# Two routings cut into lists of small steps, and gathers and first splits tied to dense groups, in a fused attention and two-MoE kernel

## The chip, the cores and the metric

The kernel runs on one core of one Trainium2 chip. The metric is the device time of one execution in microseconds (us). The engines are named as in the profile: PE multiplies matrices, ACT applies activation functions and copies, DVE and POOL work elementwise, SP issues DMAs. Each engine works through its own queue in order, and engines wait for each other by semaphores. POOL also issues the indirect DMAs (gathers and scatters).

## The reference

```python
attn_out = phi(q) (phi(k)^T v) / (phi(q) z + 1e-6)       # phi(x) = [exp(p), exp(-p)], p = x w_phi - max|x w_phi|
x = attn_out laid out as 2304 x 512
x = (silu(x @ w_gate) * (x @ w_val)) @ w_out             # first MoE: one dense block, 512 -> 1536 -> 512
logits = x @ w_gate2; e = argmax(logits)                 # second MoE: 8 experts, each token goes to one
out[token] = gate_weight * sigmoid((x @ w_output_gate)[e]) * (relu(x @ w1[e]) @ w2[e])
```

## The kernel before

Attention runs unit by unit and is woven into the first MoE by a planned order. The first MoE works on 6 blocks of 384 tokens (`n`), each in 12 slices (`f`) of the hidden width. A slice is three dense groups on PE: `mm_gv(n, f, 0)` (12 products of 128x384, called G here), `mm_gv(n, f, 1)` (the same for the value half, V) and `mm_o` of the slice before (9 products of 128x512, called o here). Every product is made of two-part numbers, so each weight is split: ACT makes the high part (L520) and POOL the low part (L524), three uses ahead, in a ring of four buffers. Between the groups, ACT takes the tanh (L547), DVE multiplies G (L550) and V (L553), ACT cuts the high part (L556) and DVE the low part (L559) for o. G and V have one PSUM bank each, so the next slice's G waits for L550, and the next V for L559.

The second MoE sorts the tokens by expert into slots of 128 rows. Slots 0 to 7 hold only tokens of blocks 0 to 4, so that they can start early: while PE is in block 5, `route_early` counts the tokens by expert (DVE), `slot_map` makes the row lists of the slots (PE, DVE), `gather` fetches the rows of a slot (POOL), and `load_w` fetches an expert's weights (SP). After block 5, `route_late` does the same for the remaining tokens, beside the first slots. Per slot there are `xt` (transpose of the gathered rows), `l1` (first layer, four chunks of weights), `ht`, and `l2` (four chunks). `Chunks.split` cuts each chunk of 128x1024 weights into two parts: ACT L889 the high one, DVE L890 the low one, in a ring of five.

The small steps are kept in a list `todo`, and `fill(1)` runs one entry of it after a dense group; an entry that is one big function is emitted as a whole. Emission is not execution: outside the planned order a scheduler places the instructions, by their data dependencies and the place in the program. In the program of before it put the four gathers of slots 0 to 3 in a row on POOL, and the first three weight splits of slot 0 into the middle of block 5, though gathers 1, 2, 3 and these splits are emitted at different places:

```python
todo += [(totals, (EARLY_T,)), (route_early, ()), (load_w, (0, 0)),
         (idle, ()), (idle, ()), (early, ())]
```

Of the kernel before, what the change touches and what calls it, by code (L numbers as in the profile page):

```python
# [13 lines left out]
AF = mybir.ActivationFunctionType  # L14
ALU = mybir.AluOpType
# [7 lines left out]
NTILE = NT // P  # L23
# [7 lines left out]
NES = 8  # L31
NLS = 17
# [149 lines left out]
def kernel(ctx, tc, qT, kT, v1, wphi, w1cat, wlog, mw1, mw2, consts, out):  # L182
    nc = tc.nc
    PE, ACT, DVE, POOL, SP = nc.tensor, nc.scalar, nc.vector, nc.gpsimd, nc.sync
# [21 lines left out]
    cv = {}  # L206
# [15 lines left out]
    IDX = buf(NES + NLS).bitcast(I32)  # L222
# [3 lines left out]
    NSI = EXI[:, 28:32]  # L226
    TKE = buf(8)
    S1, S2, S3, S4 = (buf(NTILE) for _ in range(4))
    NB, E1, E2, E3, E4 = (buf(8) for _ in range(5))
# [16 lines left out]
    T1, T2, T3 = (A[:, st + 464 + i * 312:st + 776 + i * 312] for i in range(3))  # L246
# [18 lines left out]
    x2d = dp.tile([NT, ROW], F32, name="x2d")  # L265
# [194 lines left out]
    for u in range(QSW, 16):  # L460
# [3 lines left out]
        x = qk(u + 1)  # L464
# [66 lines left out]
    def gv_mm(n, f, which):  # L531
        ps = PS[:, GB + which, :BT]
        i = where[n, f, which]
        wh, wl = WH[i % 4], WL[i % 4]
        for k in range(4):
            c = slice(k * P, (k + 1) * P)
            xh, xl = XH[:, n % 3, k, :], XL[:, n % 3, k, :]
            PE.matmul(ps, wh[:, c], xh, start=(k == 0), stop=False)  # L538
            PE.matmul(ps, wh[:, c], xl, start=False, stop=False)  # L539
            PE.matmul(ps, wl[:, c], xh, start=False, stop=(k == 3))  # L540

    def mm_gv(n, f, which):
        gv_mm(n, f, which)
# [152 lines left out]
    def bc(ap, n):  # L696
        return ap.rearrange("p (j o) -> p j o", o=1).to_broadcast([P, ap.shape[1], n])

    def bm(ap, n):
        return ap.rearrange("p (o e) -> p o e", o=1).to_broadcast([P, n, ap.shape[1]])  # L700

    def v3(ap, j, e):
        return ap[:, :j * e].rearrange("p (j e) -> p j e", e=e)

    def tt(out_, a, b, op):
        DVE.tensor_tensor(out=out_, in0=a, in1=b, op=op)

    def rsum(out_, a):
        DVE.tensor_reduce(out=out_, in_=a, axis=AX.X, op=ALU.add)
# [65 lines left out]
    def excl(out_, a):  # L775
        w = v3(T1, 8, 8)
        tt(w, cv["m8"].rearrange("p (e f) -> p e f", f=8), bm(a, 8), ALU.mult)
        rsum(out_, w)

    def pick(out_, a, nt):  # L780
        w = v3(T1, nt, 8)
        tt(w, OH[:, 0:nt, :], bm(a, nt), ALU.mult)
        rsum(out_, w)
# [6 lines left out]
    def slot_columns(q, nt, ns, valid):  # L790
        ng = 3 if valid else 2
        eq = v3(T1, nt, ns)
        tt(eq, bm(cv["iota"][:, 0:ns], nt), bc(q, ns), ALU.is_equal)
        q2 = Q2[:, :nt * ng * ns].rearrange("p (j g s) -> p j g s", g=ng, s=ns)
        DVE.tensor_scalar(out=q2[:, :, 0, :], in0=eq, scalar1=cv["pidx"], scalar2=None, op0=ALU.mult)
        tt(q2[:, :, 1, :], eq, bc(cv["jidx"][:, 0:nt], ns), ALU.mult)
        if valid:
            DVE.tensor_copy(q2[:, :, 2, :], eq)
# [16 lines left out]
    def experts(ends, ns, s0):  # L815
        w = v3(T1, ns, 8)
        tt(w, bm(ends, ns), bc(cv["iota"][:, s0:s0 + ns], 8), ALU.is_le)
        rsum(EXF[:, s0:s0 + ns], w)
        DVE.tensor_scalar(out=EXF[:, s0:s0 + ns], in0=EXF[:, s0:s0 + ns], scalar1=7.0, scalar2=None, op0=ALU.min)
        DVE.tensor_copy(EXI[:, s0:s0 + ns], EXF[:, s0:s0 + ns])  # L820
        a = max(s0, 2)
        tt(T3[:, a:s0 + ns], EXF[:, a:s0 + ns], EXF[:, a - 2:s0 + ns - 2], ALU.not_equal)
        DVE.tensor_copy(CHI[:, a:s0 + ns], T3[:, a:s0 + ns])

    EARLY_T = 15

    def route_early():
        nt = EARLY_T
        w = v3(T1, 8, 18)
        tt(w, bc(NB, 18), bm(cv["thge"], 8), ALU.is_ge)  # L830
        rsum(E1, w)
        excl(E2, E1)
        DVE.tensor_scalar(out=E3, in0=E2, scalar1=-1.0, scalar2=float(NES), op0=ALU.mult, op1=ALU.add)
        DVE.scalar_tensor_tensor(out=TKE, in0=E3, scalar=0.0, in1=E1, op0=ALU.max, op1=ALU.min)
        tt(E4, E2, TKE, ALU.add)
        experts(E4, NES, 0)
        q, tk, ge, r = S1[:, 0:nt], S2[:, 0:nt], S3[:, 0:nt], RK[:, 0:nt]
        pick(q, E2, nt)
        pick(tk, TKE, nt)
        tt(ge, r, tk, ALU.is_ge)  # L840
        tt(q, q, r, ALU.add)
        DVE.scalar_tensor_tensor(out=q, in0=ge, scalar=1000.0, in1=q, op0=ALU.mult, op1=ALU.add)
        slot_columns(q, nt, NES, False)

    def route_late():
        nt = NTILE
        w = v3(T1, 8, 18)
        tt(w, bc(NB, 18), bm(cv["thgt"], 8), ALU.is_gt)
        rsum(E1, w)
        tt(E1, E1, TKE, ALU.subtract)  # L850
        excl(E2, E1)
        tt(E3, E2, E1, ALU.add)
        DVE.tensor_copy(NSI[:, 0:1], E3[:, 7:8])
        DVE.tensor_scalar(out=E4, in0=E3, scalar1=float(NES), scalar2=None, op0=ALU.add)
        experts(E4, NLS, NES)
        tt(E2, E2, TKE, ALU.subtract)
        q, tk, lt, r = S1[:, 0:nt], S2[:, 0:nt], S3[:, 0:nt], RK[:, 0:nt]
        pick(q, E2, nt)
        pick(tk, TKE, nt)
        tt(lt, r, tk, ALU.is_lt)  # L860
        tt(q, q, r, ALU.add)
        DVE.scalar_tensor_tensor(out=q, in0=lt, scalar=1000.0, in1=q, op0=ALU.mult, op1=ALU.add)
        slot_columns(q, nt, NLS, True)


    R = [A[:, offs["KR"]:offs["KR"] + 8192], A[:, offs["WR"]:offs["WR"] + 8192]]
# [10 lines left out]
    XG = []  # L877
    HB, HTB, XB, YB = [3, 4], [5, 6], 7, [0, 1]

    class Chunks:  # L880
# [3 lines left out]
        def split(self, n):  # L884
            while self.done < min(n, len(self.seq)):
                s, c = self.seq[self.done]
                src = R[s % 2][:, c * 1024:(c + 1) * 1024]
                h, l = RG[self.done % NR]
                ACT.activation(h, src, AF.Copy)  # L889
                DVE.tensor_tensor(out=l, in0=src, in1=h.bitcast(F32), op=ALU.subtract)  # L890
                self.done += 1

# [4 lines left out]
    def load_w(s, part):  # L897
        e = SP.value_load(EXI[0:1, s:s + 1], min_val=0, max_val=NE - 1)
        src = (mw1 if part == 0 else mw2)[ds(e, 1)].rearrange("o p c -> (o p) c")
        kw = {}  # L900
        if s >= 2:
            kw["cond"] = SP.value_load(CHI[0:1, s:s + 1], min_val=0, max_val=1)
        SP.dma_start(out=R[s % 2][:, part * 4096:(part + 1) * 4096], in_=src, **kw)

    def gather(s):
        rows = EARLY_T * P if s < NES else NT
        POOL.indirect_dma_start(out=XG[s % 4], out_offset=None, in_=x2d[0:rows, :],
                                in_offset=IndirectOffsetOnAxis(ap=IDX[:, s:s + 1], axis=0),
                                bounds_check=rows - 1, oob_is_err=False)

    def xt(s):
        ps = PS[:, XB, :]
# [99 lines left out]
    def post(n):  # L1012
        ops = []
        for t in range(3):
            ops += [(post_log, (n, t)), (post_mm, (n, t))]
        return ops + [(route_a, (n,)), (route_b, (n,))]

    def early():
        slot_map(EARLY_T, NES, 0, False)
        t = ov.tile([P, OVN], F32, name="ov_gather", tag="ov")  # L1020
        for s in range(4):
            XG.append(t[:, s * 520:s * 520 + ROW])
            POOL.memset(XG[s], 0.0)
        gather(0)
        gather(1)
        load_w(0, 1)

    def idle():
        pass

    def fill(n):
        while todo and n > 0:
# [4 lines left out]
    todo = []  # L1037
    for n in range(1, NBLK):
        s0, s1 = pos[0], max(need[n], pos[0])
        for f in range(NFT):  # L1040
            def pace(g):
                run_to(s0 + ((s1 - s0) * (3 * f + g) + 35) // 36)
                if g != 2 or n == 5:
                    fill(1)
            mm_gv(n, f, 0)
            act_g(n, f)
            pace(1)
            mm_gv(n, f, 1)
            act_v(n, f)
            pace(2)  # L1050
            if prev is not None:
                mm_o(*prev)
                if prev[1] == NFT - 1:
                    for t in range(3):
                        post_x2(prev[0], t)
                    todo += post(prev[0])
                    if prev[0] == 4:
                        todo += [(totals, (EARLY_T,)), (route_early, ()), (load_w, (0, 0)),
                                 (idle, ()), (idle, ()), (early, ())]
            prev = (n, f)  # L1060
            pace(3)
            if n == 5 and f == 10:
                xt(0)
            if n == 5 and f == 10:
                load_w(1, 0)
                load_w(1, 1)
    mm_o(*prev)
    for t in range(3):
        post_x2(5, t)
    state["banks"] = [2]  # L1070
    todo += post(5) + [(totals, (NTILE,)), (route_late, ()), (idle, ()), (slot_map, (NTILE, NLS, NES, True))]
    ch = Chunks()

    def mid(n):
# [54 lines left out]
```

## Time and profile before

| | |
|---|---|
| device time, median of 3 runs | 920.05 us (918.99 to 921.12) |
| profiled execution, its own time | 920.25 us |
| span of the profile | 918.5 us |
| PE busy | 894.5 us (97%) |
| DVE busy | 577.0 us (63%) |
| ACT busy | 559.4 us (61%) |
| POOL busy | 393.0 us (43%) |

PE products overlap in the profile: one 128x512 product shows as about 0.40 us, and the next starts 0.23 us after it. So PE counts as busy as soon as products follow each other, and lost time is read from the distance between two starts.

### The profile page before, as it was taken

What the parts mean: (1) busy time and instruction counts of PE and PEld (TensorE: products, weight loads), DVE (VectorE), ACT (ScalarE), POOL (GpSimd) and SP (SyncE); (2) the same over time, 40 slices, a digit from 0 to 9 for tenths busy, and PEclk for the clock granted to TensorE, in tenths of its full rate; (3) what the DMA queues carried; (4) which work ended last, traced back from release to release, by engine and by line L of the source; (5) the groups of instructions that cost most, each with busy time, mean ns of one, the idle gap of its engine ahead of it and who ended that gap; (6) DMA issues with size and microseconds to landing.
All of it is one profiled execution on the core that took longest, in us unless ns stands there. A gap on an engine that the chain in (4) does not pass through costs nothing. (4 is left out here: it accounts for less than half of the span.)

```text
span 918.5 us, 18395 instructions
## 1 busy us (share of the span) xinstructions
PE 894.5 (97%) x7256; PEld 784.8 (85%) x7258; DVE 577.0 (63%) x977; ACT 559.4 (61%) x975; POOL 393.0 (43%) x318
## 2 busy tenths in 40 slices
PE   8899999999999999999999999979999999999995
PEld 6789989999998998898899999969877888888884
DVE  6999776443336435445433422772699988888993
ACT  5878775544353545544444444334688899888883
POOL 1667989445543434433345566566101111112200
PEclk9999999999999999999999999999999999999998
DMA  8767543200020111110000000090001147166240
GB/s 231 221 176 216 168 143 101 62 16 1 2 76 5 38 42 27 50 42 1 2 2 35 1 1 35 2 375 39 35 24 48 47 161 284 30 224 228 64 172 10
DMA packets 20940, 78.90 MB, mean 86 GB/s; under 512 B 5358, under 2 KB 5614, under 8 KB 19056
## 3 DMA queue, kind: packets, MB, share of 16 engines
q1 hardware_dynamic: 17280, 67.60, 22.8%
q0 software_dynamic: 3200, 9.48, 3.1%
q8 instruction: 59, 0.97, 0.4%
q10 hardware_dynamic: 368, 0.59, 0.3%
q14 instruction: 33, 0.27, 0.1%
HBM read 123.23 MB, written 10.00 MB: 145 GB/s over the span
## 5 line engine op out<-in xcount | busy, mean ns | idle before, releaser
L524 POOL TENSOR_TENSOR arena_r<-arena,arena_r 128x512 fp32r<-128x512 f32 x216 | 278.7, 1294 | 246.7 <-ACT arena_r L520 239.3
L520 ACT ACTIVATE arena_r<-arena 128x512 fp32r<-128x512 f32 x216 | 136.2, 631 | 229.3 <-PE banks L539 139.7
L538 PE MATMUL banks<-arena_r 128*128 128x384 f32 x576 | 202.4, 351 | 4.2 <-DVE arena L550 4.1
L890 DVE TENSOR_TENSOR arena_r<-arena,arena_r 128x1024 fp32r<-128x1024 f32 x160 | 193.1, 1255 | 20.3 <-ACT arena_r L889 18.9
L540 PE MATMUL banks<-arena_r 128*128 128x384 f32 x576 | 194.2, 337 | 0.0
L539 PE MATMUL banks<-arena_r 128*128 128x384 f32 x576 | 193.9, 337 | 0.0
L889 ACT ACTIVATE arena_r<-arena 128x1024 fp32r<-128x1024 f32 x160 | 161.9, 1067 | 18.4 <-PE banks L924 10.9
L550 DVE SCALAR_TENSOR_TENSOR arena<-arena,banks 128x384 f32<-128x384 f32 x72 | 39.7, 552 | 130.1 <-ACT arena L547 129.8
L924 PE MATMUL banks<-arena_r 128*128 128x512 f32 x480 | 117.0, 396 | 0.0
L538 PEld LDWEIGHTS banks<-arena_r 128*128 128x128 f32 x576 | 108.6, 189 | 9.5 <-DVE arena L550 4.9
L952 POOL DMA_INDIRECT out_dram<-arena x20 | 20.7, 1037 | 218.9 <-ACT arena L951 218.9
L539 PEld LDWEIGHTS banks<-arena_r 128*128 128x128 f32 x576 | 108.9, 189 | 1.2
L540 PEld LDWEIGHTS banks<-arena_r 128*128 128x128 f32 x576 | 108.7, 189 | 0.0
L924 PEld LDWEIGHTS banks<-arena_r 128*128 128x128 f32 x480 | 88.2, 188 | 20.3 <-ACT arena_r L916 2.1
L576 PE MATMUL banks<-arena_r 128*128 128x512 f32 x216 | 87.6, 405 | 0.0
L577 PE MATMUL banks<-arena_r 128*128 128x512 f32 x216 | 85.1, 394 | 1.0 <-POOL arena_r L524 1.0
L578 PE MATMUL banks<-arena_r 128*128 128x512 f32 x216 | 84.9, 394 | 0.0
L553 DVE TENSOR_TENSOR banks<-arena,banks 128x384 f32<-128x384 f32 x72 | 40.4, 561 | 44.8 <-PE banks L540 44.1
L946 PE MATMUL banks<-arena_r 128*128 128x512 f32 x160 | 62.7, 392 | 1.0 <-ACT arena_r L889 0.7
L948 PE MATMUL banks<-arena_r 128*128 128x512 f32 x160 | 62.4, 390 | 0.0
L947 PE MATMUL banks<-arena_r 128*128 128x512 f32 x160 | 62.4, 390 | 0.0
L318 DVE TENSOR_REDUCE arena<-banks 128x6 f32<-128x768 f32 x48 | 45.8, 954 | 23.6 <-PE banks L310 22.7
(119 smaller groups left out, 1327.2 us busy)
## 6 DMA issues: line engine op xcount, KB each, us to landing
arena<-mw SPq DMA_DIRECT2D x40, 2048.0 KB
ov_conv<-w1cat SPq DMA_DIRECT2D x24, 512.0 KB
arena<-w1cat SPq DMA_DIRECT2D x12, 512.0 KB
arena<-v SPq DMA_DIRECT2D x16, 325.0 KB
x2d<-arena SPq DMA_DIRECT2D x18, 256.0 KB
arena<-qT SPq DMA_DIRECT2D x15, 288.0 KB
arena<-kT SPq DMA_DIRECT2D x15, 288.0 KB
ov_gather<-x2d,arena POOLq DMA_INDIRECT x20, 4.3
```

The lines of the kernel that those rows point to most:

```text
L520: ACT.activation(WH[i % 4], WR[f][w], AF.Copy)
L524: POOL.tensor_tensor(out=WL[i % 4], in0=WR[f][w], in1=WH[i % 4].bitcast(F32), op=ALU.subtract)
L538: PE.matmul(ps, wh[:, c], xh, start=(k == 0), stop=False)
L539: PE.matmul(ps, wh[:, c], xl, start=False, stop=False)
L540: PE.matmul(ps, wl[:, c], xh, start=False, stop=(k == 3))
L576: PE.matmul(ps, GH[f % 2][:, ts_], woh, start=(f == 0), stop=False)
L577: PE.matmul(ps, GH[f % 2][:, ts_], wol, start=False, stop=False)
L578: PE.matmul(ps, GL[f % 2][:, ts_], woh, start=False, stop=(f == NFT - 1))
L889: ACT.activation(h, src, AF.Copy)
L890: DVE.tensor_tensor(out=l, in0=src, in1=h.bitcast(F32), op=ALU.subtract)
L924: PE.matmul(PS[:, HB[h], :], lhs, w[:, h * 512:(h + 1) * 512], start=a, stop=b)
L946: PE.matmul(ps, HTH[:, k, :], wh[:, cs], start=(k == 0), stop=False)
```

## The change

`tt` returns its instruction. `gv_mm` stores the last product of each dense G or V group in `state["pe"]`, and `tie(x)` gives the scheduler (not the chip: there is no semaphore in it) an order, x after that product. `route_early` and `route_late` no longer emit their steps in one call but return lists of small functions that `fill` runs one by one; the early list also holds `totals` and the load of slot 0's first weights. Three of the early steps are tied. Gathers 1, 2 and 3 are tied, and gather 1 is no longer emitted with gather 0 but in slice 10 of block 5, with the loads of slot 1. The high parts of slot 0's first three chunks are tied, so they come after block 5's last V group.

```diff
-            PE.matmul(ps, wl[:, c], xh, start=False, stop=(k == 3))
+            state["pe"] = PE.matmul(ps, wl[:, c], xh, start=False, stop=(k == 3)).ins
...
+    def tie(x):
+
+        tc.add_manual_dep(x.ins, state["pe"].name, mybir.DependencyInfo(
+            mybir.DependencyClass.NoSync, mybir.DependencyReason.SCHED_ONLY), reason="pace")
...
     def route_early():
+
         nt = EARLY_T
-        w = v3(T1, 8, 18)
-        tt(w, bc(NB, 18), bm(cv["thge"], 8), ALU.is_ge)
...
+        def counts():
+            w = v3(T1, 8, 18)
+            tie(tt(w, bc(NB, 18), bm(cv["thge"], 8), ALU.is_ge))
+            rsum(E1, w)
+            excl(E2, E1)
...
+        def picks():
+            pick(q, E2, nt)
+            pick(tk, TKE, nt)
...
+        return [(totals, (nt,)), (counts, ()), (taken, ()), (experts, (E4, NES, 0)), (load_w, (0, 0)), (picks, ()),
+                (place, ()), (slot_columns, (q, nt, NES, False))]
...
+        return [(totals, (nt,)), (counts, ()), (ends, ()), (experts, (E4, NLS, NES)), (picks, ()), (place, ()),
+                (slot_columns, (q, nt, NLS, True)), (idle, ()), (slot_map, (nt, NLS, NES, True))]
...
-                ACT.activation(h, src, AF.Copy)
+                a = ACT.activation(h, src, AF.Copy)
+                if s == 0 and c < 3:
+                    tie(a)
...
+        if 1 <= s <= 3:
+            tie(g)
...
         gather(0)
-        gather(1)
         load_w(0, 1)
...
-                        todo += [(totals, (EARLY_T,)), (route_early, ()), (load_w, (0, 0)),
-                                 (idle, ()), (idle, ()), (early, ())]
+                        todo += route_early() + [(idle, ()), (idle, ()), (early, ())]
...
             if n == 5 and f == 10:
+                gather(1)
                 load_w(1, 0)
                 load_w(1, 1)
...
-    todo += post(5) + [(totals, (NTILE,)), (route_late, ()), (idle, ()), (slot_map, (NTILE, NLS, NES, True))]
+    todo += post(5) + route_late()
```

The queue of DVE, in the middle of the early routing, reads so before (L706 is the helper `tt`, L709 a row sum, L820 and L823 the casts of `experts`, L842 the last step before `slot_columns`):

```order
L819 TENSOR_SCALAR arena<-arena 128x8
L706 TENSOR_TENSOR arena<-arena 128x120
L820 CAST arena<-arena 128x8
L706 TENSOR_TENSOR arena<-arena 128x6
...
L706 TENSOR_TENSOR arena<-arena 128x15
L842 SCALAR_TENSOR_TENSOR arena<-arena 128x15
L706 TENSOR_TENSOR arena<-arena 128x120
L550 SCALAR_TENSOR_TENSOR arena<-arena,banks 128x384
```

And so with the change, where line numbers have moved (L824, L825, L828 are the steps that were L819, L820, L823; L714 is the row sum):

```order
L824 TENSOR_SCALAR arena<-arena 128x8
L706 TENSOR_TENSOR arena<-arena 128x120
L550 SCALAR_TENSOR_TENSOR arena<-arena,banks 128x384
L825 CAST arena<-arena 128x8
L706 TENSOR_TENSOR arena<-arena 128x6
L714 TENSOR_REDUCE arena<-arena 128x15
L828 CAST arena<-arena 128x6
L706 TENSOR_TENSOR arena<-arena 128x120
L706 TENSOR_TENSOR arena<-arena 128x15
L553 TENSOR_TENSOR banks<-arena,banks 128x384
L714 TENSOR_REDUCE arena<-arena 128x15
L559 TENSOR_TENSOR arena_r<-banks,arena_r 128x384
```

The dense step L550 moved ahead of ten small steps (L820 to the last 128x120 product), and the rest of the routing now stands between the dense steps of two further slices.

POOL's queue from the clearing of the gather buffers on, before:

```order
L1023 MEMSET ov_gather 128x516 x4
L524 TENSOR_TENSOR arena_r<-arena,arena_r 128x512 x54
L907 DMA ov_gather<-x2d,arena 128x516 x4
L524 TENSOR_TENSOR arena_r<-arena,arena_r 128x512 x17
L952 DMA out_dram<-arena 2304x512
```

With the change (L936 is the gather, L983 the scatter):

```order
L1054 MEMSET ov_gather 128x516 x4
L524 TENSOR_TENSOR arena_r<-arena,arena_r 128x512 x59
L936 DMA ov_gather<-x2d,arena 128x516
L524 TENSOR_TENSOR arena_r<-arena,arena_r 128x512 x10
L936 DMA ov_gather<-x2d,arena 128x516
L524 TENSOR_TENSOR arena_r<-arena,arena_r 128x512 x2
L936 DMA ov_gather<-x2d,arena 128x516 x2
L983 DMA out_dram<-arena 2304x512
```

Gather 0 moved behind five more low parts (L524), gather 1 behind fifteen, and gathers 2 and 3 behind all seventeen.

ACT's queue at the end of block 5, before; of the splits L889, three stand further up, in the middle of the block:

```order
L547 ACTIVATE arena<-banks 128x384
L889 ACTIVATE arena_r<-arena 128x1024 x2
L556 ACTIVATE arena_r<-banks 128x384
L714 ACTIVATE arena<-banks 128x512 x3
L889 ACTIVATE arena_r<-arena 128x1024 x3
```

With the change (L916 is the split, L719 the copy of block 5's result):

```order
L547 ACTIVATE arena<-banks 128x384
L916 ACTIVATE arena_r<-arena 128x1024 x2
L556 ACTIVATE arena_r<-banks 128x384
L916 ACTIVATE arena_r<-arena 128x1024 x3
L719 ACTIVATE arena<-banks 128x512 x3
L916 ACTIVATE arena_r<-arena 128x1024 x3
```

Three splits more now stand here, ahead of the copies; DVE's low parts follow in the same order.

## Rows read from the trace of the kernel before

**Rows 1.** Windows: busy us of each engine (instructions), PEclk, DMA share, GB/s

```profile
598.00:622.00 24.00, 18.84 (x100) 16.42 (x99) 17.04 (x20) 9.16 (x16) 15.17 (x12) 0.93 0.96 393
618.10:621.30 3.20, 3.20 (x11) 3.20 (x11) 0.89 (x2) 1.01 (x2) 1.28 (x1) 0.50 0.99 415
```

**Rows 2.** Timeline (start, length, what, idle before), PE, two ordinary slices apart

```profile
625.77 0.33 PE L538 MATMUL banks<-arena_r 128*128 128x384 f32 x1
...
638.30 0.33 PE L538 MATMUL banks<-arena_r 128*128 128x384 f32 x1
```

**Rows 3.** Timeline, the early routing on DVE and the first gap

```profile
596.72 0.16 DVE L820 CAST arena<-arena 128x8 int32<-128x8 f32 x1
...
597.37 1.31 POOL L524 TENSOR_TENSOR arena_r<-arena,arena_r 128x512 fp32r<-128x512 f32 x1 [0.79 <-ACT arena_r L520]
...
597.79 0.93 DVE L706 TENSOR_TENSOR arena<-arena 128x15 f32<-128x15 f32 x1
...
598.43 0.40 PE L578 MATMUL banks<-arena_r 128*128 128x512 f32 x1
...
599.16 0.55 DVE L550 SCALAR_TENSOR_TENSOR arena<-arena,banks 128x384 f32<-128x384 f32 x1
...
599.76 0.45 PE L538 MATMUL banks<-arena_r 128*128 128x384 f32 x1 [0.94 <-DVE arena L550]
```

**Rows 4.** Timeline, the products of the slot lists, and the first gather on POOL

```profile
601.96 0.54 PE L804 MATMUL banks<-arena 128*128 128x16 bf16 x15
...
604.61 1.25 POOL L907 DMA_INDIRECT ov_gather<-x2d,arena  x1 [0.33 <-DVE arena L813]
```

**Rows 5.** Timeline, the other gaps of PE and what DVE and POOL did

```profile
608.56 0.34 PE L540 MATMUL banks<-arena_r 128*128 128x384 f32 x1
...
609.03 0.44 PE L538 MATMUL banks<-arena_r 128*128 128x384 f32 x1
...
610.60 6.70 DVE L890 TENSOR_TENSOR arena_r<-arena,arena_r 128x1024 fp32r<-128x1024 f32 x1 [0.25 <-ACT arena_r L889]
...
611.23 0.40 PE L576 MATMUL banks<-arena_r 128*128 128x512 f32 x1
611.24 4.97 POOL L524 TENSOR_TENSOR arena_r<-arena,arena_r 128x512 fp32r<-128x512 f32 x4
612.58 0.50 PE L577 MATMUL banks<-arena_r 128*128 128x512 f32 x1 [0.95 <-POOL arena_r L524]
...
614.07 0.40 PE L577 MATMUL banks<-arena_r 128*128 128x512 f32 x1
614.30 0.39 PE L578 MATMUL banks<-arena_r 128*128 128x512 f32 x1
...
617.82 0.56 PE L538 MATMUL banks<-arena_r 128*128 128x384 f32 x1 [3.13 <-DVE arena L550]
```

**Rows 6.** Timeline, PE, the first product of the group after that

```profile
621.58 0.34 PE L538 MATMUL banks<-arena_r 128*128 128x384 f32 x1
```

**Rows 7.** Timeline, DVE, the V half of an ordinary slice

```profile
642.68 0.56 DVE L553 TENSOR_TENSOR banks<-arena,banks 128x384 f32<-128x384 f32 x1 [0.60 <-PE banks L540]
...
643.81 0.56 DVE L559 TENSOR_TENSOR arena_r<-banks,arena_r 128x384 fp32r<-128x384 f32 x1 [0.56 <-ACT arena_r L556]
```

**Rows 8.** Timeline, DVE and ACT where block 5 ends

```profile
649.94 2.36 DVE L890 TENSOR_TENSOR arena_r<-arena,arena_r 128x1024 fp32r<-128x1024 f32 x2
...
652.21 0.55 DVE L559 TENSOR_TENSOR arena_r<-banks,arena_r 128x384 fp32r<-128x384 f32 x1
...
653.43 1.57 ACT L714 ACTIVATE arena<-banks 128x512 f32<-128x512 f32 x3 [2.20 <-PE banks L578]
...
655.83 0.69 DVE L723 COPY arena<-banks 128x512 f32<-128x512 f32 x1 [3.06 <-PE banks L722]
```

**Rows 9.** DMA issues from 598 to 622 us (count, median us to landing)

```profile
ov_gather<-x2d,arena POOLq DMA_INDIRECT x4, 11.4
```

**Rows 10.** Timeline, PE, the transposes of slot 1

```profile
661.38 0.66 PE L914 MATMUL banks<-arena,ov_gather 128*128 128x128 f32 x4
```

More of the change, by code (lines that the diff above doesn't have):

```diff
@@ L705, in tt @@
     def tt(out_, a, b, op):
-        DVE.tensor_tensor(out=out_, in0=a, in1=b, op=op)
+        return DVE.tensor_tensor(out=out_, in0=a, in1=b, op=op)
+    def tie(x):
+        tc.add_manual_dep(x.ins, state["pe"].name, mybir.DependencyInfo(
+            mybir.DependencyClass.NoSync, mybir.DependencyReason.SCHED_ONLY), reason="pace")
     def rsum(out_, a):
@@ L825, with idle @@
     EARLY_T = 15
+    def idle():
+        pass
     def route_early():
         nt = EARLY_T
-        w = v3(T1, 8, 18)
-        tt(w, bc(NB, 18), bm(cv["thge"], 8), ALU.is_ge)
[L831 to L836, printed above, removed]
-        q, tk, ge, r = S1[:, 0:nt], S2[:, 0:nt], S3[:, 0:nt], RK[:, 0:nt]
@@ L838, in route_early @@
[L838 to L843, printed above, removed]
+        q, tk, ge, r = S1[:, 0:nt], S2[:, 0:nt], S3[:, 0:nt], RK[:, 0:nt]
+        def counts():
[3 more added lines that the diff above has]
+            excl(E2, E1)
@@ new lines, in taken, with place @@
+        def taken():
+            tie(DVE.tensor_scalar(out=E3, in0=E2, scalar1=-1.0, scalar2=float(NES), op0=ALU.mult, op1=ALU.add))
+            DVE.scalar_tensor_tensor(out=TKE, in0=E3, scalar=0.0, in1=E1, op0=ALU.max, op1=ALU.min)
+            tt(E4, E2, TKE, ALU.add)
+        def picks():
+            pick(q, E2, nt)
+            pick(tk, TKE, nt)
+        def place():
+            tie(tt(ge, r, tk, ALU.is_ge))
+            tt(q, q, r, ALU.add)
+            DVE.scalar_tensor_tensor(out=q, in0=ge, scalar=1000.0, in1=q, op0=ALU.mult, op1=ALU.add)
@@ L845, in route_late @@
+        return [(totals, (nt,)), (counts, ()), (taken, ()), (experts, (E4, NES, 0)), (load_w, (0, 0)), (picks, ()),
+                (place, ()), (slot_columns, (q, nt, NES, False))]
     def route_late():
         nt = NTILE
[L847 to L854, printed above, removed]
@@ L855, in route_late, with counts @@
-        experts(E4, NLS, NES)
-        tt(E2, E2, TKE, ALU.subtract)
-        q, tk, lt, r = S1[:, 0:nt], S2[:, 0:nt], S3[:, 0:nt], RK[:, 0:nt]
[L858 to L863, printed above, removed]
+        q, tk, lt, r = S1[:, 0:nt], S2[:, 0:nt], S3[:, 0:nt], RK[:, 0:nt]
+        def counts():
+            w = v3(T1, 8, 18)
+            tt(w, bc(NB, 18), bm(cv["thgt"], 8), ALU.is_gt)
+            rsum(E1, w)
+            tt(E1, E1, TKE, ALU.subtract)
+            excl(E2, E1)
@@ new lines, in ends, with picks, place @@
+        def ends():
+            tt(E3, E2, E1, ALU.add)
+            DVE.tensor_copy(NSI[:, 0:1], E3[:, 7:8])
+            DVE.tensor_scalar(out=E4, in0=E3, scalar1=float(NES), scalar2=None, op0=ALU.add)
+        def picks():
+            tt(E2, E2, TKE, ALU.subtract)
+            pick(q, E2, nt)
+            pick(tk, TKE, nt)
+        def place():
+            tt(lt, r, tk, ALU.is_lt)
+            tt(q, q, r, ALU.add)
+            DVE.scalar_tensor_tensor(out=q, in0=lt, scalar=1000.0, in1=q, op0=ALU.mult, op1=ALU.add)
@@ L906, in gather @@
         rows = EARLY_T * P if s < NES else NT
-        POOL.indirect_dma_start(out=XG[s % 4], out_offset=None, in_=x2d[0:rows, :],
-                                in_offset=IndirectOffsetOnAxis(ap=IDX[:, s:s + 1], axis=0),
-                                bounds_check=rows - 1, oob_is_err=False)
+        g = POOL.indirect_dma_start(out=XG[s % 4], out_offset=None, in_=x2d[0:rows, :],
+                                    in_offset=IndirectOffsetOnAxis(ap=IDX[:, s:s + 1], axis=0),
+                                    bounds_check=rows - 1, oob_is_err=False)
+        if 1 <= s <= 3:
+            tie(g)
     def xt(s):
@@ L1024, in early @@
         gather(0)
-        gather(1)
         load_w(0, 1)
-    def idle():
-        pass
     def fill(n):
```

## Prediction

> **What bounds the kernel now.** I read the busy time by stretch first, then the timeline of the stretch that stood out, on every engine. From 598 to 622 us PE works 18.84 of 24.00 us [rows 1], though in the ordinary slices behind it one product follows the other. What such a slice costs: two G groups, two slices apart, start at 625.77 and 638.30 [rows 2], so a slice takes 6.265 us. Two 128x512 products start 0.23 apart (614.07, 614.30 [rows 5]); nine of them are 2.07, which leaves 4.195 for the 24 products of 128x384, 0.175 each. So the kernel is bound by PE, and the change can only win what PE loses in places, above all in these 24 us.
>
> PE loses it five times there, each read as the distance of two starts less the ordinary one:
> 1. 598.43 to 599.76, where G waits for DVE's L550 [rows 3]: 1.33 - 0.23 = 1.10.
> 2. 608.56 to 609.03 [rows 5]: 0.47 - 0.175 = 0.30.
> 3. 611.23 to 612.58, where o waits for POOL's low part [rows 5]: 1.12.
> 4. 614.30 to 617.82, again for L550 [rows 5]: 3.29.
> 5. From 617.82 to 621.58 twelve products take 3.76 [rows 5, 6] where 2.10 is ordinary: 1.66. PEclk is 0.50 in that stretch [rows 1], the lower of the two levels (1.2 GHz instead of 2.4), right behind the gap of number 4.
>
> Together 7.47. Counted over the whole stretch: had the G group of 598.66 (598.43 + 0.23) started at once, then three slices of 6.265 and the 15 list products (0.54 at most [rows 4]) would lie ahead of the group at 625.77. 598.66 + 18.80 + 0.54 = 618.00, so 7.77; with 0.4 for the list, since products overlap, 7.91. The difference to 7.47 is the slow first product after each gap. I take 7.8.
>
> **Why PE waits there.** The first gap is order alone: ten small routing steps stand ahead of L550 in DVE's queue, which starts at 599.16, while the first of the ten starts at 596.72 [rows 3].
>
> The others come from the gathers and the early splits together. POOL has its first gather at 604.61 [rows 4] and returns to low parts at 611.24 [rows 5]: 6.63 us for four gathers, 1.66 each, in which no weight is split. Then it runs four low parts without a pause, 4.97 us. DVE's third weight split starts at 610.60 and lasts 6.70 us, where its fellows take 1.18 (2.36 for two [rows 8]). It ends after POOL's four, and L550 stands behind it.
>
> This is more than bad order. A DVE step that reads only SBUF stands still while POOL works on SBUF operands: a 128x15 step of 0.93 us at 597.79 ends at 598.72, and POOL's low part, started at 597.37, ends at 598.68 [rows 3]. DVE's dense steps that read PSUM aren't held like this: L550 takes 0.55 there, and L553 and L559 take 0.56 [rows 3, 7].
>
> The Trainium skill, "SBUF — State Buffer", section "SBUF: two separate sides", says that a DVE step with two SBUF inputs and a POOL step share a port pair, that whichever starts first keeps it for its whole instruction, and that the other fully blocks. The 0.93 agrees. By that rule a split would lose one turn, some 1.24 us, and gap 4 would be about 3.7 us shorter; the row shows it losing four turns in a row. The measurement decides.
>
> **The change part by part.**
>
> *Routing in small steps.* L550 moves ahead of the ten steps, to where L820 started, 596.72, and is done by 597.3; G wants to start at 598.66. Gap 1 goes: -1.10. The ten steps and the rest of the routing now delay L553 and L559 instead, and the next V waits for those. The steps ahead of L553 took 1.07 us (596.72 to 597.79 [rows 3]). Begun at 597.2, with one step held by the low part that ends at 598.68, L553 starts between 598.2 and 599.0. From L553 to the end of L559 an ordinary slice needs 643.81 + 0.56 - 642.68 = 1.69 [rows 7], so the end is at 599.9 to 600.7. V starts twelve products behind 598.66, at 600.76. It just holds, so I take 0; a second turn lost to POOL would cost 1.31 less what margin there is, at most 1.3.
>
> The slot lists come two slices later: same products, same cost, 0. The late routing stands on DVE in the order of before, step for step beside the same splits: 0.
>
> *Gathers.* Gather 0 alone holds POOL for 1.66. Four in a row took 6.63 and PE lost 1.12 by them, so a cover of about 5.5 lies over POOL; one gather at a time is hidden, and gathers 2 and 3 stand behind the last low part, where POOL has no dense work. The backlog of four low parts does not form: -1.12. Gather 0 waits for the slot list as before, but both have moved by five low parts. If it came to the head of POOL before the list, POOL would stand; the same 5.5 covers that.
>
> *First splits.* Three splits leave the middle of block 5, and with them ACT's wait for slot 0's weights in front of dense work: -0.30 and -3.29, and with gap 4 the slow clock, -1.66. The Trainium skill, "TensorE: Matmul & The Clock Gate", section "Part 1: The HAM clock gate (the "warmup" mystery)", says that the slow state is the default and activity releases it. The 0.50 right behind the gap [rows 1] agrees.
>
> What they cost: three low parts, 3 x 1.18 = 3.54 us of DVE, arrive where block 5 ends, and ACT's three high parts stand ahead of the copies of block 5 (653.43 before [rows 8]). Their cover: DVE stands idle for 3.06 us ahead of the copy at 655.83, waiting for PE's transposes [rows 8]. DVE's second half, L559, ends at 652.76; three splits later it is 656.3, half a us beyond 655.83. Meanwhile PE has slot 0's first layer, whose chunks come ready one after the other, and the first needs none but the first split, which runs right behind L553. The copies would come about 1 us later, and PE's queue has nine products instead of six ahead of the first transposes, which fills 0.7 of it. I take +0.3, between 0 (all covered) and 3.54 (no cover), near the cover, since it is an actual idle time on the same engine at the same place.
>
> *SP.* The load of slot 2's first weights now stands behind the three writes of block 5, some 5 us later; it is needed two slots on: 0.
>
> *Sum.* 920.25 (the profiled execution's own time) - 7.8 + 0.3 = 912.75. That execution lies 0.20 above the median of the runs, so I predict **912.6**.
>
> **The rivals.**
>
> *The small steps hold up V.* For it: the margin at V is 0.1 to 0.9 us, and each of some 20 steps can lose a turn to a low part. Against it: each slice has 1 to 2 us of margin of its own. Price: one to two lost turns, 1.3 each less the margin, so about 914.0.
>
> *Block 5's end takes it back.* The splits are exposed there: +3.5 instead of +0.3, 916.0. For it: ACT and DVE are in-order, and copies and dense steps stand behind the splits. Against it: the 3.06 idle.
>
> *It changes nothing.* The stall returns because another backlog forms behind gather 0 while steps of the routing wait at the port; with gaps 3 to 5 still there only the 1.4 of gaps 1 and 2 is won: 919. Against it: no split of 1.18 stands in DVE's queue any more in this stretch.
>
> *A gather comes late: slower than before.* Gather 1 came second behind 604.61 [rows 4], and its transposes ran at 661.38 [rows 10]. Now gather 0 stands five low parts later, one per dense group of some 2.1 us, so at about 615, and gather 1 ten more behind it, at about 636. With 7.8 us won its transposes come at 653.6, so it has 17.6 us. Against it: the landing took 11.4 in the median while the weights were loading [rows 9], and in the new place nothing loads. Beyond 17.6 + 7.8 = 25.4 us of landing the kernel is slower; at 30 it would be about 924.
>
> **How the numbers follow.** The main case 0.74 (its own range 911.5 to 913.8), V held up 0.10, the end of block 5 0.08, nothing 0.04, late gather 0.04. A difference below 0.2%, 1.84 us, is about what a measurement of this kernel can't tell from none, so faster is below 918.2. The first three cases are faster: 0.92; the case that changes nothing is 0.03 same and 0.01 slower, which with the late gather makes 0.05 slower. For 8 in 10 the range takes the main case and V held up whole and part of block 5's end: 911.3 to 915.2.
>
> **What would show it.** Right: PE without gaps from 598 to 648 us, PEclk 1.00 there, no DVE step of several us, L550 always ahead of its G, gathers apart on POOL, and block 5's last o about 7.8 us earlier, first-layer products following it without a gap over 0.3. Wrong: a V product that waits for L559 near 600 us, an L706 of over 2 us, first-layer products that wait for L919, or transposes that wait for a gather.

## The result, and the profile after

The changed kernel takes 911.45 us in the median of 4 runs (911.37 to 911.61). The kernel before took 919.52 beside it (918.58 to 921.12). The ratio is 0.9914, with a 95% interval of 0.9901 to 0.9926. So the change is a gain of 8.1 us, or 0.9%; the forecast was 912.6, and the time lies at the low end of its range of 911.3 to 915.2.

The profiled execution took 911.40 us, with a span of 909.6. I read it in the order of the prediction: first the stretch in which PE lost time before [rows 1], as windows.

```profile
598.00:622.00 24.00, 24.00 (x142) 22.52 (x141) 11.71 (x24) 10.32 (x19) 15.95 (x13) 1.00 0.89 362
```

PE is busy for 24.00 of 24.00 us where it was for 18.84, and PEclk is 1.00 instead of 0.93. DVE's share fell from 17.04 to 11.71: the splits are gone from here. The timeline of PE dates the gain.

```profile
598.26 0.39 PE L578 MATMUL banks<-arena_r 128*128 128x512 f32 x1
598.49 0.33 PE L538 MATMUL banks<-arena_r 128*128 128x384 f32 x1
...
600.59 0.33 PE L538 MATMUL banks<-arena_r 128*128 128x384 f32 x1
...
630.31 0.33 PE L538 MATMUL banks<-arena_r 128*128 128x384 f32 x1
```

The first row is the product that stood at 598.43 before [rows 3], the last the G group that stood at 638.30 [rows 2]. From one to the other it was 39.87 us and is 32.05. So **the stretch gave 7.82 us** (the forecast was 7.8). G follows its predecessor by 0.23, so gap 1 is gone.

DVE in the same place, where the routing is now in pieces:

```profile
596.54 0.54 DVE L550 SCALAR_TENSOR_TENSOR arena<-arena,banks 128x384 f32<-128x384 f32 x1
...
597.35 1.17 DVE L828 CAST arena<-arena 128x6 int32<-128x6 f32 x1
...
598.71 0.55 DVE L553 TENSOR_TENSOR banks<-arena,banks 128x384 f32<-128x384 f32 x1
...
599.82 0.56 DVE L559 TENSOR_TENSOR arena_r<-banks,arena_r 128x384 fp32r<-128x384 f32 x1 [0.38 <-ACT arena_r L556]
...
602.19 0.77 DVE L706 TENSOR_TENSOR arena<-arena 128x15 f32<-128x15 f32 x1
...
603.55 1.37 DVE L706 TENSOR_TENSOR arena<-arena 128x120 f32<-128x120 f32 x1
```

L550 starts 2.62 us earlier than before (599.16). The cast L828 has only six columns and takes 1.17 us, where it took 0.15 before: it stands still until a low part of POOL ends at 598.49 (597.20 + 1.29, the first row of the next fence). L559 ends at 600.38, and V starts at 600.59. The margin that the prediction worked out was there, but only 0.2 us of it was left. In the next slice two more steps lose a turn (0.77 and 1.37); L559 still ends before V wants to start.

The gathers on POOL, and their landing in the list of DMA issues from 598 to 645 us:

```profile
597.20 1.29 POOL L524 TENSOR_TENSOR arena_r<-arena,arena_r 128x512 fp32r<-128x512 f32 x1 [0.79 <-ACT arena_r L520]
...
613.64 1.26 POOL L936 DMA_INDIRECT ov_gather<-x2d,arena  x1 [0.33 <-DVE arena L818]
...
634.65 1.02 POOL L936 DMA_INDIRECT ov_gather<-x2d,arena  x1 [0.15 <-issue]
...
638.98 1.01 POOL L936 DMA_INDIRECT ov_gather<-x2d,arena  x1
640.29 1.00 POOL L936 DMA_INDIRECT ov_gather<-x2d,arena  x1 [0.30 <-issue]
```

```profile
ov_gather<-x2d,arena POOLq DMA_INDIRECT x4, 3.4
```

The gathers stand apart, take 1.0 to 1.3 us each, and land after 3.4 us in the median. Gather 1 thus lands some 14 us before slot 1's transposes at 652.65 (further below). Then the end of block 5, DVE and ACT:

```profile
641.94 2.36 DVE L919 TENSOR_TENSOR arena_r<-arena,arena_r 128x1024 fp32r<-128x1024 f32 x2
644.22 0.55 DVE L559 TENSOR_TENSOR arena_r<-banks,arena_r 128x384 fp32r<-128x384 f32 x1
644.69 3.49 DVE L919 TENSOR_TENSOR arena_r<-arena,arena_r 128x1024 fp32r<-128x1024 f32 x3
648.45 0.69 DVE L728 COPY arena<-banks 128x512 f32<-128x512 f32 x1 [0.28 <-PE banks L727]
```

```profile
645.98 1.55 ACT L719 ACTIVATE arena<-banks 128x512 f32<-128x512 f32 x3
```

L559 starts at 644.22, which is 652.21 - 7.99: the splits don't delay it, because ACT's L556 stands behind two of them as before. DVE's copy comes 7.38 earlier than before instead of 7.99 [rows 8], so 0.6 late, and it waits 0.28 where it waited 3.06. PE doesn't see it, as its next rows show no idle time:

```profile
645.70 2.22 PE L955 MATMUL banks<-arena_r 128*128 128x512 f32 x9
647.75 0.60 PE L727 MATMUL banks<-arena 128*128 128x128 f32 x4
648.10 1.18 PE L955 MATMUL banks<-arena_r 128*128 128x512 f32 x4
...
652.65 0.27 PE L945 MATMUL banks<-arena,ov_gather 128*128 128x128 f32 x1
```

One gap remains in the last stage, where PE waits for a split of ACT. The last of the four products in the first row starts at 682.47 (681.66 + 1.20 - 0.39) and the next at 683.58, 0.88 more than the ordinary 0.23. The kernel before had this gap too, 8 us later and of the same size.

```profile
681.66 1.20 PE L955 MATMUL banks<-arena_r 128*128 128x512 f32 x4
...
683.58 0.49 PE L977 MATMUL banks<-arena_r 128*128 128x512 f32 x1 [0.72 <-ACT arena_r L916]
```

### The profile page after: what moved, and what is told of

The parts are those of the page before. It is cut to its first block, busy times and chain, and to the rows that moved or that the text cites. A ratio compares the mean times of both kernels' runs of the same rounds, so it can differ in the third digit from the quotient of the medians.

```text
span 909.6 us, 18394 instructions
## 1 busy us (share of the span) xinstructions
PE 891.7 (98%) x7258; PEld 783.3 (86%) x7258; DVE 572.8 (63%) x977; ACT 559.3 (61%) x975; POOL 391.5 (43%) x318
## 5 line engine op out<-in xcount | busy, mean ns | idle before, releaser
L524 POOL TENSOR_TENSOR arena_r<-arena,arena_r 128x512 fp32r<-128x512 f32 x216 | 278.6, 1293 | 242.4 <-ACT arena_r L520 234.9
L919 DVE TENSOR_TENSOR arena_r<-arena,arena_r 128x1024 fp32r<-128x1024 f32 x160 | 187.3, 1220 | 17.7 <-ACT arena_r L916 16.5
L916 ACT ACTIVATE arena_r<-arena 128x1024 fp32r<-128x1024 f32 x160 | 161.7, 1066 | 14.7 <-PE banks L955 10.4
L550 DVE SCALAR_TENSOR_TENSOR arena<-arena,banks 128x384 f32<-128x384 f32 x72 | 39.7, 552 | 131.9 <-ACT arena L547 131.7
L983 POOL DMA_INDIRECT out_dram<-arena x20 | 20.6, 1032 | 216.3 <-ACT arena L982 216.3
L553 DVE TENSOR_TENSOR banks<-arena,banks 128x384 f32<-128x384 f32 x72 | 40.3, 560 | 45.4 <-PE banks L540 45.0
```

The lines of the kernel that those rows point to most:

```text
L524: POOL.tensor_tensor(out=WL[i % 4], in0=WR[f][w], in1=WH[i % 4].bitcast(F32), op=ALU.subtract)
L916: a = ACT.activation(h, src, AF.Copy)
```

## The experiments

My theory (A): gaps 3 to 5, some 6 of the 7.8 us, need two things at once, a backlog on POOL and a split in DVE's queue, because POOL steps without a pause between them shut DVE out; gap 1 is order alone. Rival B: the splits alone stall DVE. Rival C: the gathers alone make the gaps. (In e9 and e10, theory B is another one, told there.) To compare kernels I use, beside the times, **the length of the stretch**: from the last product ahead of gap 1 to the G group of [rows 2] that stood at 638.30. It is read from one profiled execution of each kernel and leaves out what scatters at the start and the end.

| kernel | median us | ratio to before (95%) | stretch us |
|---|---|---|---|
| before | 919.1 beside e1 to e4, 919.6 beside e5 to e8 | | 39.87 |
| the change | 911.45 | 0.9914 (0.9901 to 0.9926) | 32.05 |
| e1, without the split tie | 911.16 | 0.9911 (0.9894 to 0.9927) | 32.06 |
| e2, without the gather tie | 912.09 | 0.9926 (0.9910 to 0.9943) | 32.04 |
| e3, without the routing lists | 912.18 | 0.9920 (0.9903 to 0.9936) | 33.26 |
| e4, gather tie alone | 913.20 | 0.9934 (0.9915 to 0.9953) | 33.72 |
| e5, split tie alone | 913.37 | 0.9929 (0.9914 to 0.9945) | 33.28 |
| e6, routing lists alone | 912.68 | 0.9922 (0.9907 to 0.9937) | 33.85 |
| e7, before with pauses on POOL | 914.10 | 0.9941 (0.9926 to 0.9956) | 34.84 |
| e8, the change, late routing spread | 911.14 | 0.9910 (0.9896 to 0.9924) | 32.05 |

**e1_no_split_tie.** The change without the tie of slot 0's first splits.

```diff
-                a = ACT.activation(h, src, AF.Copy)
-                if s == 0 and c < 3:
-                    tie(a)
+                ACT.activation(h, src, AF.Copy)
```

> The changed kernel without the tie on the first three weight splits, which return to the middle of block 5 (two of their low parts ahead of L550 on DVE). Theory A (a split stalls only behind a backlog of low parts on POOL, and the backlog needs four gathers in a row): no backlog, so each split loses at most one turn of 1.3 us to POOL, within the margin; 911.5 to 913.0. Rival B (the splits alone stall DVE, by waiting for weights in front of dense steps): gap 4 and the slow clock return, 916 or more. Rival C (the gathers alone made the gaps): 911.4, no DVE step above 2 us.

The stretch is as short as with the tie. The splits return to the middle of block 5 and do no harm there (timeline, DVE):

```profile
607.48 1.23 DVE L917 TENSOR_TENSOR arena_r<-arena,arena_r 128x1024 fp32r<-128x1024 f32 x1 [1.31 <-ACT arena_r L916]
608.95 1.99 DVE L917 TENSOR_TENSOR arena_r<-arena,arena_r 128x1024 fp32r<-128x1024 f32 x1 [0.25 <-ACT arena_r L916]
...
611.98 1.22 DVE L917 TENSOR_TENSOR arena_r<-arena,arena_r 128x1024 fp32r<-128x1024 f32 x1
```

One of them loses one turn (1.99). The time lies 0.3 below the range of A, and B is refuted; C expected what was measured, so this run does not separate it from A, and e2 and e5 have to. One thing is not as A says: POOL has a backlog here too, four low parts without a pause, but they lose turns to the splits as well (7.55 us, where four took 4.97 before [rows 5]).

```profile
608.04 7.55 POOL L524 TENSOR_TENSOR arena_r<-arena,arena_r 128x512 fp32r<-128x512 f32 x4 [3.04 <-ACT arena_r L520]
```

**e2_no_gather_tie.** The change without the tie of the gathers, and with gather 1 behind gather 0 again.

```diff
-        if 1 <= s <= 3:
-            tie(g)
...
         gather(0)
+        gather(1)
...
-                gather(1)
```

> The changed kernel with gather 1 emitted right behind gather 0 again and no tie on gathers 1 to 3: POOL has gathers 0, 1, 2 in a row, one low part, and gather 3. Theory A: the gap of PE for a late low part returns (1.1 us or a bit less, since three in a row hold POOL 5.0 us and not 6.6), but no split is on DVE, so no gap of 3 us and no slow clock: 911.6 to 912.6. Rival B: 911.4. Rival C: most of the loss returns, 916 to 918.

The gathers come nearly in a row again (timeline, POOL), and PE still has no gap:

```profile
613.79 1.26 POOL L936 DMA_INDIRECT ov_gather<-x2d,arena  x1 [0.32 <-DVE arena L818]
615.36 1.01 POOL L936 DMA_INDIRECT ov_gather<-x2d,arena  x1 [0.31 <-issue]
616.67 1.00 POOL L936 DMA_INDIRECT ov_gather<-x2d,arena  x1 [0.30 <-issue]
617.69 1.31 POOL L524 TENSOR_TENSOR arena_r<-arena,arena_r 128x512 fp32r<-128x512 f32 x1
619.16 1.01 POOL L936 DMA_INDIRECT ov_gather<-x2d,arena  x1 [0.16 <-issue]
```

A gather takes 1.0 to 1.3 here, not the 1.66 that the prediction took from four of them. The gap of 1.1 that A expected for a late low part did not come, and C, with 916 to 918, is refuted.

**e3_no_routing_lists.** Both ties stay; the two routings are emitted in one call each, as before.

```diff
-                        todo += route_early() + [(idle, ()), (idle, ()), (early, ())]
+                        todo += [(totals, (EARLY_T,)), (route_early, ()), (load_w, (0, 0)),
+                                 (idle, ()), (idle, ()), (early, ())]
```

> The changed kernel with both routings in one call each, as before the change; gathers and splits stay tied. Theory A: only the first gap returns, 1.1 us, since L550 stands behind ten routing steps again: 912.3 to 912.7. Rival (the lists matter for where the list products and the gathers stand, so more than the first gap returns): 913.5 or more.

Only gap 1 is back: G starts 1.34 after the product ahead of it, 1.11 more than ordinary. The stretch is longer by 1.21. PE rows of the timeline:

```profile
598.47 0.40 PE L578 MATMUL banks<-arena_r 128*128 128x512 f32 x1
599.81 0.45 PE L538 MATMUL banks<-arena_r 128*128 128x384 f32 x1 [0.94 <-DVE arena L550]
```

**e4_gather_tie_alone, e5_split_tie_alone, e6_routing_lists_alone.** The kernel before with one part of the change each: the gather tie (with gather 1 moved), the tie of the first splits, or the lists (whose early steps hold the three ties of routing steps).

```diff
+        if 1 <= s <= 3:
+            tie(g)
```

```diff
+                if s == 0 and c < 3:
+                    tie(a)
```

```diff
+                        todo += route_early() + [(idle, ()), (idle, ()), (early, ())]
```

> The kernel before with the gathers alone moved and tied; splits in the middle of block 5 and routing in one call as before. Theory A: gap 1 (1.1) stays, gap 2 (0.3) may stay, gaps 3 to 5 (6.1) go: 6 us below the kernel before, 912.7 to 914. Rival B: gap 4 stays with the slow clock, about 918. Rival C: the same as theory A here.

> The kernel before with the tie on the first three weight splits alone; routing in one call, gathers 0, 1, 2 in a row and gather 3 behind one low part. Theory A: with no split in DVE's queue there, a backlog on POOL hurts nobody, so gap 1 (1.1) alone stays: 912 to 913. Rival C (the gathers make the gaps by themselves): gap 3 and a part of gap 4 stay, 914.5 or more.

> The kernel before with the routings as lists and their ties alone; splits in the middle of block 5, gathers 0, 1, 2 in a row, a low part, gather 3. The lists put the gathers five low parts later, behind the splits. Theory A: splits and backlog no longer meet in time, so gaps 1 to 5 all go, or one turn stays: 911 to 912.5. Rival (order alone, a split or a gather in a row costs wherever it is): gap 4 stays, 915 or more.

Each part alone takes 6.0 to 6.6 us out of the stretch, nearly all of the 7.82. Alone they add up to 18.8 us. So **the parts are substitutes, not addends**. The times of e5 and e6 lie 0.4 and 0.2 above the ranges of A, and e4's lies within. In e5 POOL has its backlog with no split beside it, and gap 1 alone is left, which C did not allow; e6 pays two small waits for low parts behind its gathers (0.71 and 0.43) but not gap 1. The timeline of POOL in e5:

```profile
611.32 6.28 POOL L524 TENSOR_TENSOR arena_r<-arena,arena_r 128x512 fp32r<-128x512 f32 x5
```

Five low parts follow each other without a pause (five take 6.28, where one takes 1.28 to 1.30), and nothing waits for it.

In e4 and e6 the backlog is there as well, with splits beside it: six low parts without a pause in e4, four in 7.55 us in e6. Yet each split loses at most one turn (at most 2.32 and 2.00), because the two engines take turns. The timeline of e4, first POOL's six, then, each by itself, two splits on DVE and the low parts that stood still for them:

```profile
607.37 10.03 POOL L524 TENSOR_TENSOR arena_r<-arena,arena_r 128x512 fp32r<-128x512 f32 x6 [1.75 <-ACT arena_r L520]
...
608.64 1.62 DVE L898 TENSOR_TENSOR arena_r<-arena,arena_r 128x1024 fp32r<-128x1024 f32 x1
609.20 2.21 POOL L524 TENSOR_TENSOR arena_r<-arena,arena_r 128x512 fp32r<-128x512 f32 x1
610.18 2.32 DVE L898 TENSOR_TENSOR arena_r<-arena,arena_r 128x1024 fp32r<-128x1024 f32 x1
611.38 2.26 POOL L524 TENSOR_TENSOR arena_r<-arena,arena_r 128x512 fp32r<-128x512 f32 x1
```

So a backlog and a split in DVE's queue are not enough for the long stall. In the kernel before, the chain of low parts began behind a gather, ahead of a split that was already waiting, and no low part stood still.

**e7_pause_on_pool.** The kernel before, with a clearing step of 128x8 on POOL ahead of each low part in the middle of block 5; gathers, splits and routing are untouched.

```diff
         n, f, w = uses[i]
+        if n == 5 and 4 <= f <= 8:
+            POOL.memset(WL[i % 4][:, 0:8].bitcast(F32), 0.0)
```

> The kernel before with a small memset on POOL ahead of each low part of slices 4 to 8 of block 5, so that POOL's low parts behind the gathers don't all start before the one ahead has ended; the output is the same. Theory A in its narrow form (DVE lost four turns since POOL's next step starts before the last has ended, and gets in at the first pause): the split of 6.70 us is below 3 us, gap 4 below 1 us, no slow clock; 914 to 916.5. Rival D (the split was held by something else, such as the gathers or the weights' transfer): still above 5 us, 919 or more.

The long split shrinks from 6.70 to 3.02 us, just above the 3 that was expected (timeline; DVE and POOL, lines moved by two):

```profile
610.99 3.02 DVE L892 TENSOR_TENSOR arena_r<-arena,arena_r 128x1024 fp32r<-128x1024 f32 x1 [0.25 <-ACT arena_r L891]
613.93 0.54 DVE L552 SCALAR_TENSOR_TENSOR arena<-arena,banks 128x384 f32<-128x384 f32 x1
```

```profile
611.64 1.28 POOL L526 TENSOR_TENSOR arena_r<-arena,arena_r 128x512 fp32r<-128x512 f32 x1
612.85 0.16 POOL L525 MEMSET arena_r<- 128x8 f32 x2
613.04 2.12 POOL L526 TENSOR_TENSOR arena_r<-arena,arena_r 128x512 fp32r<-128x512 f32 x1
```

The split loses the last gather and one low part, gets in during the clearing steps, and now the next low part stands still for it (2.12 instead of 1.28). Gap 4 is gone, and PEclk is 1.00 from 598 to 648 us; gaps 1 and 3 remain (1.16 and 1.13). So pauses alone bring back 5.0 of the 7.8 us. That gap 3 stays shows that it does not come from the chain: the low part that PE waits for is the first behind the gathers, and two of the four gathers last 1.91 and 1.53 beside the splits before (1.69 and 1.53 here), where 1.0 is ordinary. That is 1.4 too much, more than the 1.12 of the gap (an estimate; no run takes the splits away and keeps four gathers in a row). Whether a short POOL step that also reads SBUF would let DVE in, as this one does, which only writes, no run shows.

**e9_probe_in_the_chain, e10_probe_with_pauses.** Was it the chain of low parts, or the gather that the split began to wait behind? e9 puts one DVE step on SBUF operands into e5's chain, where no gather is near; its result is never read. e10 adds the pauses. One run each.

```diff
         g_lo(f)
+        if (n, f) == (5, 6):
+            DVE.tensor_tensor(out=GP, in0=GP, in1=GL[f % 2].bitcast(F32), op=ALU.add)
```

```diff
+        if n == 5 and 6 <= f <= 8:
+            POOL.memset(WL[i % 4][:, 0:8].bitcast(F32), 0.0)
```

> This is the kernel with the split tie alone, in which POOL runs five low parts without a pause from about 611.3 to 617.6 us and no split stands in DVE's queue, plus one DVE step of 128x384 that reads and writes SBUF only, right behind the L559 that ends at about 613.0 (its result is overwritten by the next L550 and never read, so the output is the same). Theory A (a chain of POOL steps without a pause shuts a waiting DVE step out to the chain's end, whatever it began to wait behind): the step starts at about 613.0 and ends about half a us behind the fifth low part, at 618.1, so it lasts about 5.0 us, and the L550 behind it starts at about 618.0 instead of 616.46. Theory B (each lets the other in after one whole instruction, and the four turns lost before had to do with the gather that the split began to wait behind): it is held by one low part only, ends at about 614.4 and lasts at most 1.4 us. The time is that of the split tie alone within 0.5 us in either case, since the next G group starts only at 619.5.

> The same with a small clearing step (128x8) on POOL ahead of each low part of slices 6 to 8 of block 5, which breaks the chain of low parts. Theory A: the step gets in at the first break, so it lasts at most 1.9 us (one low part and its own half a us), and a low part behind it takes some 0.5 us longer than 1.29. Theory B: the same length as without the pauses.

Timeline of e9, DVE and POOL, and then of e10:

```profile
612.92 4.98 DVE L570 TENSOR_TENSOR arena<-arena,arena_r 128x384 f32<-128x384 f32 x1
618.01 0.56 DVE L550 SCALAR_TENSOR_TENSOR arena<-arena,banks 128x384 f32<-128x384 f32 x1
...
611.20 6.28 POOL L524 TENSOR_TENSOR arena_r<-arena,arena_r 128x512 fp32r<-128x512 f32 x5
```

```profile
612.99 1.49 DVE L572 TENSOR_TENSOR arena<-arena,arena_r 128x384 f32<-128x384 f32 x1
...
614.01 0.10 POOL L525 MEMSET arena_r<- 128x8 f32 x1
614.18 1.45 POOL L526 TENSOR_TENSOR arena_r<-arena,arena_r 128x512 fp32r<-128x512 f32 x1
```

In e9 the step lasts 4.98 us and ends 0.42 behind the chain (611.20 + 6.28 = 617.48). In e10 it gets in at the first clearing step behind it and lasts 1.49; the low part behind it is held for 0.16 us, not for the 0.5 that was expected. So a chain of low parts can shut a DVE step out to its end without a gather that it began to wait behind. Neither costs time (912.89 and 912.95, and both stretches are 33.26), because in e9 the L550 that starts 1.6 us later than in e5 still ends 0.8 us ahead of its G group.

**e8_late_routing_spread.** The change, with two empty entries ahead of each step of the late routing, against the 0.88 that is left.

```diff
-    todo += post(5) + route_late()
+    todo += post(5)
+    for step in route_late():
+        todo += [(idle, ())] * 2 + [step]
```

> The changed kernel with two empty entries ahead of each step of the late routing, which then ends some two slots later. Theory: the one gap that is left in slot 2's first layer (0.88 us, a product of the second layer placed ahead of its chunk's high part while DVE is full) goes, since the products stand in the plain order again: 910.4 to 911.0, 0.5 to 0.9 below the changed kernel. Rival: the later list comes out the same, since DVE has some 5 us free per 50 and the steps hold up splits in the next slots: 911.4 or more.

The gap goes, as one row of PE shows, but the time stays within the scatter: 911.14 (910.03 to 912.50) to 911.45. It lies between the 910.4 to 911.0 of the theory and the 911.4 or more of the rival.

```profile
682.08 5.16 PE L955 MATMUL banks<-arena_r 128*128 128x512 f32 x21
```

From the G group at the stretch's end to PE's last product it takes 269.29 us instead of 269.65. So 0.36 of the 0.88 arrives. Where the rest goes I did not settle; a sign is that behind the gap DVE, too, has no idle time, as the windows of the change show:

```profile
684.00:700.00 16.00, 16.00 (x93) 13.13 (x92) 16.00 (x25) 13.29 (x16) 2.31 (x2) 1.00 0.17 51
```

## Why the prediction was right, step by step

*The stretch* (7.8): 7.82, and the gaps went one by one as said. *Gap 1* by the lists alone: shown by e3 (1.21 lost without them) and by e6. *Gaps 2 to 5*: right in size, since 6.37 was counted and e3, which lacks the lists alone, is 6.61 below the kernel before. The cause, gathers and early splits together, is right, since taking away either wins nearly all of it (e4, e5). But "the backlog of four low parts does not form" is right only for the whole change: with the gathers moved alone six low parts follow without a pause (e4), and the splits still get their turns. What the prediction did not see is that any one part would do, the lists too (e6). It gave gap 3 to the gathers and gaps 2, 4 and 5 to the splits, as if each edit had its own share; e1 and e2 show that neither tie is needed beside the other parts. *Gap 5*, the clock at 0.50 behind 3.29 us without products: in e3 to e7 PE has gaps of at most 1.2 and the clock stays at 1.00. That agrees with the lower clock following from the longer idle time; no run changes the clock alone.

*"It just holds"* at V: it held by 0.2. In place of the one lost turn that was counted, three were lost over two slices, each inside its slice's margin.

*"+0.3" where block 5 ends*: mis-sized, it cost nothing. The copy comes 0.6 late, as forecast ("half a us"), but from the G group at the stretch's end to PE's last product it was 269.79 us before and is 269.65. PE's queue of first-layer products covers all of it.

*A gather alone "holds POOL for 1.66"*: 1.0 to 1.26. The four took 1.25, 1.01, 1.91 and 1.53, the last two beside splits, and the mean of 1.66 also holds the idle time between them. It changed nothing, since it was covered. *The late gather*: landing 3.4 us against 17.6 to spare; the rival had no ground.

*The sum* was 912.75 for the profiled execution, which took 911.40, so 1.35 more was won than forecast. Of that, 0.3 and 0.14 lie at the end of block 5 and in the last stage, 0.17 ahead of the stretch, and 0.70 behind PE's last product, where it was 10.38 us to the end of the span and is 9.68. That last piece is no effect that I can name: the same tail lies between 9.3 and 10.2 in the other changed kernels, whose last stage is nearly the same.

Two readings of rows were loose. That a DVE step on SBUF operands alone stands still beside POOL holds for the 0.93 that was shown, but not for every step: the row sum L709 at 597.48 took 0.28 beside the same low part, and 0.26 at 596.87 with POOL idle. And of the steps shown as not held, L550 and L553 ran while POOL was idle; e5 shows L550 at 0.55 (616.46) and e9 L553 at 0.56 (611.21) beside low parts.

The Trainium skill, "SBUF — State Buffer", section "SBUF: two separate sides", says that the one that starts first has the shared pair for its whole instruction. The prediction worked out from it that a waiting split would lose one turn and gap 4 would be 3.7 shorter; that is more than the gap's 3.29, so it would be gone. For a single POOL step the traces agree with one turn (1.37, 1.99), and so do e4's splits among six low parts (1.62, 2.32). In the chain of e9 they differ: 4.98 for a step that began to wait during the second of five low parts. The measurement decides, as the prediction assumed.

## What to carry to other kernels

Look for a small step on DVE that lasts as long as several POOL steps: POOL work that queues up without a pause can shut a DVE step with SBUF operands out to its end, and the dense step behind it pays. Break the chain (e7), empty DVE's queue there (e5), or move what the chain begins behind (e4, e6); each took 5.0 to 6.6 of the 7.8 us by itself, so try the cheapest alone before adding the others. And compare variants by the stretch that they change, since start and tail of an execution scatter by as much as the small edits are worth.

## What the runs showed of the hardware

A DVE step of 128x384 on SBUF operands, some 0.4 us by itself (an estimate: it ended 0.42 behind the last low part), lasted 4.98 us beside five low parts on POOL without a pause, and 1.49 when a clearing step of 128x8 (0.1 us) stood between the low parts. An indirect gather takes 1.0 us on POOL by itself (1.26 for gather 0, the first of an execution), and 1.5 to 1.9 beside splits on DVE. DVE's dense steps with a PSUM operand ran at 0.56 us beside the same chain.

What decides who goes next is open. In the chains of the kernel before and of e9 POOL starts its next step some 0.04 us before the last one ends (two low parts take 2.52, one 1.28), and the waiting DVE step of 128x1024 or 128x384 gets no turn. Where a low part had itself stood still for a split (twice each in e1, e4 and e6), the waiting split got in every time, though the next low part started 0.02 to 0.03 after the end of the last in one case of each run and 0.03 to 0.04 before it in the other. Behind the last gather of the kernel before, which had stood still too (1.53), the low part came 0.02 later, and there the split lost. So neither the size of the pause nor a held POOL step ahead decides alone.
